# Fourier mix behind attention: later sines, another sign mask, sign changes on three engines, and one relay moved ahead

## The chip, the cores and the metric

The kernel runs on one core of a Trainium2 chip. The metric is the device time of one launch in microseconds (us). Its engines, as the profile names them, are TensorE (PE, its weight loads PEld), VectorE (DVE), ScalarE (ACT), GpSimd (POOL) and SyncE (SP); SP issues most of the plain stores and transposing DMAs, POOL the loads.

## The reference

Eight batches, twelve heads, 448 positions, head width 64:

```python
scores = scale * np.matmul(q, k.transpose(0, 1, 3, 2))
attn = np.maximum(scores, 0.0) ** 2 / S
x = np.matmul(attn, v)                 # heads side by side: (8, 448, 768)
u = x + np.real(np.fft.fft(np.fft.fft(x, axis=1), axis=2))
un = (u - mean(u)) / np.sqrt(var(u) + 1e-6)
out = u + np.maximum(un @ w_ch1, 0.0) @ w_ch2      # 768 -> 3072 -> 768
```

So there is an attention without softmax, a Fourier mix along positions and channels of which the real part is added, a normalization of each row, and a feed-forward part of two large products.

## The kernel before, in words

**Tiling.** Attention takes one batch after another, four heads to a group (`load_group`: q, k and v come by POOL's DMAs as bf16). For batches 0 and 1 queries and keys are turned on TensorE (`turn_on_pe`, L545 and the copy L552). From batch 2 on, DVE copies them into relay buffers `qkr` (L509), one buffer for queries and one for keys, and SP turns each by a transposing DMA into `qkT` (L521). The relay of one group is thus a q copy, a k copy and two DMAs; a relay buffer is free when its DMA has read it. Scores (L857) land in PSUM, ACT takes relu (L870) into an `sq` buffer, DVE squares it (L887; elsewhere ACT, L884), and TensorE multiplies by values (L842 in batch 0, L785 later). The result leaves PSUM as `xT` (L594 on ACT, L596 on DVE), and DVE folds each block of 128 channels with its mirror image (sum and difference, L671).

**Fourier mix.** The transforms are products with cosine and sine tables, built on the chip. For each table `turns` makes the phase as a fraction of a turn (L311, L313) and its absolute value (L315), on DVE; `sine` then has ACT take two sines (L320). There are two tables for positions (`seq`) and three for channels (`chan` 0, 1, 2); half of each channel table is needed with the sign changed, too (`chan_neg`, L361, and `nseq`, L357). In batch 0 `first_channels` multiplies six folded blocks of channels (m = 0 to 5) by the tables (L1307), in two row blocks i: blocks 0 to 2 use `chan[m]`, blocks 3 to 5 use `chan[m-3]` and `chan_neg`. Row block 1 waits for all scores of batch 0. The PSUM results are cast (`pc`, L1351), and `first_tail` does the position products (L932), the residual (L935), the statistics and the norms. Behind the last relu ACT loads another function table, for square roots (`root_table`, L367). Later batches go through `mix` (L1332, L1351) and `mix_rows` (L1147).

**Feed-forward part.** Rows are taken in groups; the first product is L1793 with a relu (L1778 DVE, L1780 ACT), the second L1821, L1848 and L1933, partly with sums of weight blocks, and L1515 adds onto the output rows. Two PSUM banks (`BF`) and three double banks (`BS`) serve all of it.

**Order of the work.** The program's order is made at build time by a planner (`Streams.run`). Each piece of work is a generator that asks with `need(engine, duration, waits, buffers)`, and issues its instructions when it is chosen. The planner always takes the piece that can start earliest by its own durations; on a tie, the smaller rank goes first, and the rank is a pair, one for TensorE and one for the other engines, given at `sch.add`. An `need("SP", 0.0, ...)` only waits in the plan and emits nothing. `warming` fills TensorE with matmuls on zeros (L2011) until batch 0's channel products are done. Each engine runs its instructions in the planned order, and waits in it for whatever its next instruction needs.

`turn_rest` plans the groups of batches 1 to 7 one after another at rank (2, 2). `others` builds channel tables 1 and 2, at 0.15 for DVE and ACT; squares have 0.2, `first_fold` 0.3, `negative` (nseq and the three sign changes) 0.35.

Of the kernel before, what the change touches and what calls it, by code (L numbers as in the profile page):

```python
# [166 lines left out]
def kernel(  # L167
# [9 lines left out]
    nc = tc.nc  # L177
# [125 lines left out]
    def build_dft():  # L303
        row, col, col2 = drow, dcol, dcol2

        def turns(f, g, cols, rows, n, i):

            d = dve(n) + 0.04
            yield need("DVE", d, [indices_ready])
            r = work.tile([128, 2 * KH], mybir.dt.int32, name="dftr", tag=f"pc{TC[i][0]}", bufs=1)  # L310
            nc.vector.tensor_scalar(r[:, :n], cols, rows, None, op0=ALU.mult)  # L311
# [3 lines left out]
            nc.vector.scalar_tensor_tensor(g, f, -1.0, f, op0=ALU.mult, op1=ALU.max)  # L315
            return e

        def sine(dst, y, n, e, sign=1, bias=zero_t):
            e = yield need("ACT", act(n), [e + LATENCY["DVE"]])
            nc.scalar.activation(dst, y, AF.Sin, bias=bias, scale=sign * 2.0 * math.pi)  # L320
            dft_ready.t = e + LATENCY["ACT"]
# [13 lines left out]
        def channel_table(m):  # L335
            y = early_hid if m == 2 else work.tile([128, 4 * KH], FP32, name="dfty", tag=("u1A", "u1B")[m], bufs=1)
            e = yield from turns(y[:, 2 * KH:4 * KH], y[:, 0:2 * KH], col2, row[:, 4 + m:5 + m], 2 * KH, m % 2)
            yield from sine(chan[m][:, 0, :], y[:, 0:2 * KH], 2 * KH, e, -1, halfpi)
            yield from sine(chan[m][:, 1, :], y[:, 2 * KH:4 * KH], 2 * KH, e)
            chan_made[m].t = dft_ready.t  # L340
# [10 lines left out]

    chan_made, dft_all = [Cell() for _ in range(3)], Cell()

    def negative():

        e = yield need("DVE", 0.35, [seq_ready])
        nc.vector.tensor_scalar(nseq, seq[:, 1], -1.0, None, op0=ALU.mult)  # L357
        nseq_ready.t = e + LATENCY["DVE"]
        for m in range(3):
            e = yield need("DVE", 0.27, [chan_made[m]])  # L360
            nc.vector.tensor_scalar(chan_neg[:, m], chan[m][:, :, KH:], -1.0, None, op0=ALU.mult)  # L361
            chan_ready[m].t = e + LATENCY["DVE"]

    def root_table():

        yield need("ACT", 1.5, [dft_all, last_relu])
        nc.scalar.activation(drow[:, 7:8], zero_t, AF.Sqrt, bias=eps_t)  # L367
# [128 lines left out]

    def turning(bs):

        for b in bs:
            for g in range(NG):  # L500
                if b < 2:
# [68 lines left out]
    def fold(b, m, F, av, give, av_end):  # L570
# [58 lines left out]
        if b == 0:  # L629
# [662 lines left out]

    first_pps, first_chan = [None, None], [Cell(), Cell()]

    def first_channels(i, ms):

        n0, n1 = TC[i]
        for m in ms:
# [4 lines left out]
            for t in range(2):  # L1303
                parts = [(0, 2 * KH, chan[m][:, t, :])] if m < 3 else \
                    [(0, KH, chan[m - 3][:, t, 0:KH]), (KH, 2 * KH, chan_neg[:, m - 3, t, :])]
                for c0, c1, tab in parts:
                    nc.tensor.matmul(first_pps[i][:n1 - n0, t, c0:c1], lhsT=first_folds[m][:, t, n0:n1], rhs=tab,  # L1307
                                     start=(i == 1 and m == 0), stop=(m == MC - 1 and c1 == 2 * KH))
        if m < MC - 1:
            sch.add(first_channels(i, [MC - 1]), (0, 0))  # L1310
        else:
# [704 lines left out]
    with tc.manual_schedule():  # L2016
# [18 lines left out]
        sch.add(root_table(), (0, 0.4))  # L2035
        sch.add(negative(), (0, 0.35))
        for slot in range(6):
# [33 lines left out]
```

## Time and profile before

| what | us |
|---|---|
| median of 3 runs (577.87 to 578.24) | 578.0 |
| the profiled execution | 577.99 |
| its span | 576.0 |
| TensorE busy | 565.0 |
| VectorE busy | 446.9 |
| ScalarE busy | 336.9 |
| GpSimd busy | 134.0 |

The span goes from the first to the last instruction of the profiled execution; its time has 1.99 us more around it. A row of a timeline reads: start, duration, engine, line, operation, output <- inputs, size, count, and in brackets how long the engine had been idle and what ended that. A merged row (x5) covers several instructions. Lines are those of the listing above.

### The profile page before, as it was taken

The numbers are of one execution on the slowest core, as the hardware profiler recorded it, in microseconds if no ns is written. First come the engines' busy times: TensorE is split into PE (matmuls) and PEld (weight loads), VectorE is DVE, ScalarE is ACT, GpSimd is POOL, SyncE is SP. The second block draws the span as 40 slices with busy tenths as digits, with TensorE's granted clock in tenths as the row PEclk, the third lists the DMA queues.
The fourth block names the chain that finished last, engine by engine and source line by source line (L and its number), as shares of the span: only waits on it lengthen the run. The fifth ranks groups of instructions, "written<-read, shape, count | busy, mean of one in ns | idle before, by whom it ended". The sixth has DMA issues, their size and how long they took to land.

```text
span 576.0 us, 11341 instructions
## 1 busy us (share of the span) xinstructions
PE 565.0 (98%) x4339; PEld 358.5 (62%) x4344; DVE 446.9 (78%) x1030; ACT 336.9 (59%) x538; POOL 134.0 (23%) x187
## 2 busy tenths in 40 slices
PE   8999999999999999999999999999999999999997
PEld 6466556544465546556757567568567786868864
DVE  6988775986688877997798879978978994267872
ACT  5977772977745676667559658856573160406400
POOL 8527102410134113321333116112220230000000
PEclk9999999999999999999999999999999999999999
DMA  9999999656938985799769977996654342223012
GB/s 125 206 211 249 202 219 181 174 109 78 202 78 223 175 140 119 161 167 193 140 136 197 201 126 161 177 173 113 141 107 94 109 142 85 66 73 93 2 41 97
DMA packets 133505, 81.84 MB, mean 142 GB/s; under 512 B 77516, under 2 KB 128716, under 8 KB 133452
## 3 DMA queue, kind: packets, MB, share of 16 engines
q0 software_dynamic: 40320, 33.63, 37.2%
q1 hardware_dynamic: 93132, 47.50, 36.6%
q8 instruction: 34, 0.56, 0.4%
q14 instruction: 19, 0.16, 0.1%
HBM read 62.91 MB, written 26.25 MB: 155 GB/s over the span
## 4 chain that ended last, share of the span: by engine, by line
PE 87%; DVE 9%; ACT 3%; issue 1%; DVEq 0%; ACTq 0%
PE psF L1793 31%; PE psF L1933 21%; PE psS L857 6%; PE psF L785 5%; PE psF L1821 4%; PE psS L1933 4%; PE psS L1635 3%; PE psF L1848 3%; PE psS L1332 2%; DVE sq L887 2%; ACT sq L870 1%; PE psS L785 1%; PE psS L2011 1%; PE psF L1635 1%; PE psS L932 1%; PE psS L1307 1%
## 5 line engine op out<-in xcount | busy, mean ns | idle before, releaser
L1793 PE MATMUL psF<-unT,w 128*128 128x256 bf16 (+2 forms) x1435 | 197.6, 294 | 1.3 <-ACT hT L1780 0.7
L870 ACT ACTIVATE sq<-psS 112x896 bf16<-112x896 f32 x192 | 165.2, 930 | 39.6 <-PE psS L857 39.2
L1793 PEld LDWEIGHTS <-w 128*128 128x128 bf16 x1440 | 137.5, 98 | 58.7 <-issue 12.9
L887 DVE TENSOR_TENSOR sq<-sq 112x896 bf16<-112x896 bf16 x163 | 98.4, 620 | 15.9 <-ACT sq L870 14.9
L1780 ACT ACTIVATE hT<-psF 128x512 bf16<-128x512 f32 (+3 forms) x144 | 71.7, 513 | 66.5 <-PE psF L1793 65.3
L1933 PEld LDWEIGHTS <-hT 128*128 128x128 bf16 x720 | 69.0, 98 | 50.3 <-issue 5.9
L1933 PE MATMUL psF<-w,hT 128*128 128x384 bf16 x378 | 67.1, 326 | 0.7 <-DVE xT L612 0.7
L1515 DVE TENSOR_TENSOR o<-psF,o 128x384 f32<-128x384 f32 x80 | 44.2, 553 | 25.2 <-PE psF L1933 20.8
L857 PE MATMUL psS<-qkT 64*128 64x448 bf16 (+1 forms) x384 | 52.8, 358 | 2.5 <-ACT sq L870 1.9
L413 POOL DMA_DIRECT2D vn<-in_v_dram x24 | 17.5, 730 | 105.4 <-PE psS L857 86.0
L1176 POOL TENSOR_TENSOR u<-tp,xn 112x385 f32<-112x385 f32 (+2 forms) x14 | 13.6, 974 | 109.0 <-DVE tp L1158 81.8
L857 PEld LDWEIGHTS <-qkT 64*128 64x128 bf16 (+1 forms) x384 | 17.3, 101 | 31.1 <-issue 24.1
L612 DVE TENSOR_SCALAR xT<-psF 128x224 bf16<-128x224 f32 x54 | 18.5, 383 | 21.8 <-PE psF L785 21.7
L785 PE MATMUL psF<-sq,vn 112*64 112x448 bf16 x264 | 31.3, 358 | 0.9 <-DVE hT L1778 0.9
L1204 ACT ACTIVATE un<-u,nmr,rstd 113x768 bf16<-113x768 f32 (+2 forms) x23 | 23.0, 1022 | 14.9 <-DVE nmr L1191 14.6
L413 POOL DMA_DIRECT2D qn<-in_q_dram x21 | 15.2, 724 | 62.7 <-DVE qkr L509 53.0
L1933 PE MATMUL psF<-wsum,hT 128*128 128x384 bf16 x162 | 28.8, 326 | 0.0
L1185 DVE BATCH_NORM_STATS2 stats<-u 112x6 f32<-112x384 f32 (+2 forms) x56 | 28.8, 540 | 0.0
L785 PEld LDWEIGHTS <-vn 112*64 112x64 bf16 x336 | 15.8, 109 | 19.6 <-issue 13.4
L884 ACT ACTIVATE sq<-sq 112x896 bf16<-112x896 bf16 x29 | 27.3, 950 | 0.5
L1821 PE MATMUL psF<-w,hT 128*128 128x384 bf16 x144 | 24.9, 326 | 0.0
L1848 PE MATMUL psF<-w,hT 128*128 128x384 bf16 x144 | 24.4, 326 | 0.0
(228 smaller groups left out, 783.2 us busy)
## 6 DMA issues: line engine op xcount, KB each, us to landing
out_dram<-o SPq DMA_DIRECT2D x56, 192.0 KB, 2.3
vn<-in_v_dram POOLq DMA_DIRECT2D x24, 224.0 KB, 5.0
qn<-in_q_dram POOLq DMA_DIRECT2D x21, 224.0 KB, 4.5
kn<-in_k_dram POOLq DMA_DIRECT2D x21, 224.0 KB, 7.3
w<-in_moe_w_ch_dram POOLq DMA_DIRECT2D x12, 384.0 KB, 13.2
w<-in_moe_w_ch_dram POOLq DMA_DIRECT2D x4, 1152.0 KB, 15.5
utop<-u SPq DMA_DIRECT2D x12, 336.0 KB, 3.8
o<-utop SPq DMA_DIRECT2D x16, 192.0 KB, 4.2
```

Source lines behind the costliest of these rows:

```text
L413: nc.gpsimd.dma_start(out=t, in_=src[b, hs].rearrange("h (p j) d -> p h (j d)", j=4))
L785: nc.tensor.matmul(av[h * Dh:(h + 1) * Dh, 0:S], lhsT=vn[:, c, h0 + h, :], rhs=sq[:, h, :], start=(c == 0), stop=(c == 3))
L857: nc.tensor.matmul(sc[:wide, h, 0:S].rearrange("k (c q) -> k c q", c=4), lhsT=flat[ps, k0:k0 + wide], rhs=qT[ps, m % 2], start=True, stop= ...
L870: nc.scalar.activation(r, sc[:R, :, 0:S], AF.Relu)
L887: nc.vector.tensor_tensor(r, r, r, op=ALU.mult)
L1185: nc.vector.bn_stats(stats[:n, hf, :], u[:n, hf * (D // 2):(hf + 1) * (D // 2)])
L1515: nc.vector.tensor_tensor(o, pc[:, 0:DH], o, op=ALU.add)
L1780: nc.scalar.activation(hs, ps, AF.Relu)
L1793: nc.tensor.matmul(ph[:, i * N:(i + 1) * N], lhsT=w1_sb[m][hf][:, (jj + i) * 128:(jj + i + 1) * 128], rhs=unT[:, m, 0:N], start=(m == 0), ...
L1821: nc.tensor.matmul(pc[:, 0:DH], lhsT=block(j, c), rhs=w2(j, hf), start=(j == 0), stop=(j == JC - 1))
L1848: nc.tensor.matmul(pc[:, 0:DH], lhsT=block(2 * i + k, c), rhs=weights[i], start=(start and i == 0), stop=(i == KP - 1), skip_group_check=True)
L1933: nc.tensor.matmul(pc[:, 0:DH], lhsT=lhs[i], rhs=rhs[i], start=(start and i == 0), stop=(i == KP - 1), skip_group_check=True)
```

## The change

- **Late sines.** Both sines of channel table 2 now also wait, in the plan, for the last relu of batch 0. The other tables' sines stay as they are.
- **Sign mask.** The absolute value of the phase is made by clearing the sign bit of the 32-bit word, an operation with one source, where it was the larger of f and −f. The planned durations change with it.
- **Moved sign changes.** `chan_neg` of table 0 stays on DVE, that of table 1 goes to POOL, that of table 2 to ACT, and the function table for square roots is loaded behind the latter. The rank of `negative` goes from 0.35 to 0.15.
- **Folds and channel products.** `first_fold` gets rank 0.2 for the engines other than TensorE. The channel products of batch 0 are planned as separate pieces: block 0, then blocks 1 to 4 in any order, and block 5 when these four are done.
- **Relay.** `turn_rest` plans batch 2's three groups one by one, each when the one ahead of it is turned. The second of them (batch 2, group 1) gets rank 0.05 for its copies, all others keep 2.

```diff
-            yield need("DVE", d, [indices_ready])
+            yield need("DVE", d - 0.14, [indices_ready])
...
-            e = yield need("DVE", d)
-            nc.vector.scalar_tensor_tensor(g, f, -1.0, f, op0=ALU.mult, op1=ALU.max)
+            e = yield need("DVE", dve2(n))
+            nc.vector.tensor_scalar(g.bitcast(mybir.dt.int32), f.bitcast(mybir.dt.int32), 0x7FFFFFFF, None, op0=ALU.bitwise_and)
...
-        def sine(dst, y, n, e, sign=1, bias=zero_t):
-            e = yield need("ACT", act(n), [e + LATENCY["DVE"]])
+        def sine(dst, y, n, e, sign=1, bias=zero_t, deps=()):
+            e = yield need("ACT", act(n), [e + LATENCY["DVE"], *deps])
...
+            deps = [last_relu] if m == 2 else []
+            yield from sine(chan[m][:, 0, :], y[:, 0:2 * KH], 2 * KH, e, -1, halfpi, deps)
+            yield from sine(chan[m][:, 1, :], y[:, 2 * KH:4 * KH], 2 * KH, e, deps=deps)
...
-            e = yield need("DVE", 0.27, [chan_made[m]])
-            nc.vector.tensor_scalar(chan_neg[:, m], chan[m][:, :, KH:], -1.0, None, op0=ALU.mult)
-            chan_ready[m].t = e + LATENCY["DVE"]
+            en = ("DVE", "POOL", "ACT")[m]
+            e = yield need(en, {"DVE": 0.27, "POOL": 0.7, "ACT": act(2 * KH)}[en], [chan_made[m]])
+            if en == "ACT":
+                nc.scalar.activation(chan_neg[:, m], chan[m][:, :, KH:], AF.Copy, scale=-1.0)
+                negated.t = e
+            else:
+                (nc.gpsimd if en == "POOL" else nc.vector).tensor_scalar(chan_neg[:, m], chan[m][:, :, KH:], -1.0, None,
+                                                                         op0=ALU.mult)
+            chan_ready[m].t = e + LATENCY[en]
...
-        yield need("ACT", 1.5, [dft_all, last_relu])
+        yield need("ACT", 1.5, [dft_all, last_relu, negated])
...
-        sch.add(turning(range(1, B)), (2, 2))
+        sch.add(turning([1], range(NG)), (2, 2))
+        yield need("SP", 0.0, [*turned_at[1][2]])
+        sch.add(turning([2], [0]), (2, 2))
+        yield need("SP", 0.0, [*turned_at[2][0]])
+        sch.add(turning([2], [1]), (2, 0.05))
+        yield need("SP", 0.0, [*turned_at[2][1]])
+        sch.add(turning([2], [2]), (2, 2))
+        yield need("SP", 0.0, [*turned_at[2][2]])
+        sch.add(turning(range(3, B), range(NG)), (2, 2))
...
-            sch.add(first_fold(m, x, f, gone.t + LATENCY["DVE"]), (0.3, 0.3))
+            sch.add(first_fold(m, x, f, gone.t + LATENCY["DVE"]), (0.3, 0.2))
...
-        if m < MC - 1:
-            sch.add(first_channels(i, [MC - 1]), (0, 0))
+        if m == 0:
+            for x in range(1, MC - 1):
+                sch.add(first_channels(i, [x]), (5, 5))
+        elif m < MC - 1:
+            channels_made[i] += 1
+            if channels_made[i] == MC - 2:
+                sch.add(first_channels(i, [MC - 1]), (0, 0))
...
-            sch.add(first_channels(i, range(MC - 1)), (5, 5))
+            sch.add(first_channels(i, [0]), (5, 5))
...
-        sch.add(negative(), (0, 0.35))
+        sch.add(negative(), (0, 0.15))
```

More of the change, by code (lines that the diff above doesn't have):

```diff
@@ L350, in build_dft @@
         sch.add(others(), (0, 0.15))
-    chan_made, dft_all = [Cell() for _ in range(3)], Cell()
+    chan_made, dft_all, negated = [Cell() for _ in range(3)], Cell(), Cell()
     def negative():
@@ L495, with turning @@
     turned_at = [[[Cell() for _ in range(2)] for _ in range(NG)] for _ in range(B)]
-    def turning(bs):
+    def turning(bs, gs=range(NG)):
         for b in bs:
-            for g in range(NG):
+            for g in gs:
                 if b < 2:
```

4 lines of the change are left out of this document (1 added, 3 removed).

## The prediction

> **What bounds the kernel now.** I read the page's busy line first, then the shares of the chain that ended last.
>
> ```profile
> PE 565.0 (98%) x4339; PEld 358.5 (62%) x4344; DVE 446.9 (78%) x1030; ACT 336.9 (59%) x538; POOL 134.0 (23%) x187
> ...
> PE 87%; DVE 9%; ACT 3%; issue 1%; DVEq 0%; ACTq 0%
> ```
>
> TensorE is busy nearly throughout, so the next view is the table of stages, TensorE alone (stretch, its length, busy time and instructions, granted clock, DMA share, GB/s), from the first feed-forward work on.
>
> ```profile
> 48.00:72.00 24.00, 22.35 (x214) 1.00 1.19 222
> 72.00:240.00 168.00, 167.72 (x1096) 1.00 0.84 154
> 240.00:348.00 108.00, 107.33 (x839) 1.00 0.91 164
> 348.00:360.00 12.00, 11.07 (x102) 1.00 0.83 182
> 360.00:528.00 168.00, 167.89 (x1323) 1.00 0.54 118
> ```
>
> In these 480 us TensorE idles 1.65 + 0.28 + 0.67 + 0.93 + 0.11 = 3.64 us, at a full granted clock. What remains is work that no part of the change removes. A gain must come from the opening, before useful TensorE work is dense (there its busy time holds filler matmuls of L2011), or out of those 3.64 us. So I read the opening, by all engines, then the timelines of ACT, DVE and PE one by one.
>
> ```profile
> 24.00:36.00 12.00, 11.07 (x74) 5.48 (x74) 11.78 (x34) 10.80 (x17) 4.08 (x7) 1.00 1.08 212
> ```
>
> The columns are PE, PEld, DVE, ACT and POOL. DVE is busy 11.78 of 12 us here. ACT's 10.80 us understate it:
>
> ```profile
> 22.12 0.73 ACT L320 ACTIVATE chan<-early,halfpi 128x386 bf16<-128x386 f32 x1
> 22.62 0.72 ACT L320 ACTIVATE chan<-early,zero_t 128x386 bf16<-128x386 f32 x1
> 23.13 6.67 ACT L870 ACTIVATE sq<-psS 112x896 bf16<-112x896 f32 x8
> ...
> 32.06 1.16 ACT L870 ACTIVATE sq<-psS 112x896 bf16<-112x896 f32 x1
> 33.24 1.28 ACT L367 ACT_TABLE_LOAD   x1
> 34.53 0.29 ACT L367 ACTIVATE drow<-zero_t,eps_t 128x1 f32<-128x1 f32 x1
> 36.90 1.05 ACT L1351 CAST pc<-psS 128x386 bf16<-128x386 f32 x2 [2.08 <-PE psS L1307]
> ```
>
> No row before the last carries an idle time: ACT runs without a gap through batch 0's last relu, which ends by 33.24, and only then idles, 2.08 us, for TensorE's first channel products (L1307). What comes behind that relu:
>
> ```profile
> 33.25 0.62 DVE L887 TENSOR_TENSOR sq<-sq 112x896 bf16<-112x896 bf16 x1
> 33.79 0.65 DVE L671 TENSOR_TENSOR fold<-xT 128x225 bf16<-128x225 bf16 x3
> 34.35 0.37 DVE L361 TENSOR_SCALAR channeg<-chan 128x386 bf16<-128x386 bf16 x1
> 34.64 0.67 DVE L596 TENSOR_SCALAR xT<-psF 128x224 bf16<-128x224 f32 x2
> 35.23 0.42 DVE L361 TENSOR_SCALAR channeg<-chan 128x386 bf16<-128x386 bf16 x2
> 35.57 0.45 DVE L671 TENSOR_TENSOR fold<-xT 128x225 bf16<-128x225 bf16 x2
> ```
>
> and TensorE, first its timeline, then two pieces of the chain that ended last:
>
> ```profile
> 34.03 0.38 PE L842 MATMUL psF<-sq,vn 112*64 112x448 bf16 x2
> ...
> 35.12 0.24 PE L1307 MATMUL psS<-channeg,fold 128*128 128x193 bf16 x1
> 35.20 0.25 PE L1307 MATMUL psS<-chan,fold 128*128 128x193 bf16 x1
> ```
> ```profile
> 34.41 2.79 PE psS L1307 x28
> 37.20 0.51 PE psF L545 x16
> ```
>
> Last relu, square (L887), last values (L842), x turned out of PSUM (L596), last fold (L671) follow each other; but TensorE still has 28 of the channel matmuls to do behind the last values, back to back to 37.20. They could not come sooner: five of the twelve folds and all three sign changes stand at the end of DVE's queue. Two things bound the opening, ACT's sum up to the last relu and this backlog.
>
> **The change, part by part.** *Late sines.* Channel table 2's two sines leave the relu run and follow the last relu. By the starts of the rows they hold ACT for 23.13 − 22.12 = 1.01 us, so the last relu ends at 33.24 − 1.01 = 32.23, if DVE frees the buffers as fast. They then run at 32.23 and 32.73 and end at 32.73 + 0.69 = 33.42 (0.69 from the row of table 1's second sine, below).
>
> *Sign mask.* `|f|` becomes a one-source operation.
>
> ```profile
> 18.42 0.69 ACT L320 ACTIVATE chan<-dfty,zero_t 128x386 bf16<-128x386 f32 x1
> ```
> ```profile
> 16.79 0.55 DVE L315 SCALAR_TENSOR_TENSOR dfty<-dfty 128x386 f32<-128x386 f32 x1
> ...
> 19.10 0.41 DVE L311 TENSOR_SCALAR dftr<-dcol,drow 128x386 int32<-128x386 f32 x1
> ```
>
> The nearest row is L311, one source of the same size: 0.41 for 0.55 us. No row has a bitwise operation; the saving lies between 0 and, at half the old price, 0.28 us an operation. I take 0.14. Of five, two stand in the full stretch behind 14 us: 0.28 us of DVE.
>
> *Moved sign changes.* Table 0's stays on DVE but goes ahead of squares. Table 1's goes to POOL, table 2's to ACT: DVE loses one or both of the 35.23 pair, which held it to 35.57, 0.34 us for two.
>
> ```profile
> 39.54 0.48 ACT L984 COPY u<-psS 128x384 f32<-128x384 f32 x1 [0.82 <-DVE stats L955]
> ```
> ```profile
> 29.88 0.53 POOL L443 DMA_DIRECT2D w<-in_moe_w_ch_dram  x1 [1.28 <-DMA w<-in_moe_w_ch_dram]
> ...
> 43.29 0.99 POOL L1005 TENSOR_SCALAR un<-u,rstd,nmr 128x768 bf16<-128x768 f32 x1 [0.76 <-DVE nmr L976]
> ```
> ```profile
> L1793 PE MATMUL psF<-unT,w x144: 322/326/337, 51.7 to 88.0; 128*128 128x384 bf16 x144
> ...
> DMA to landing us min/median/max: 6.7/13.2/19.3
> ```
>
> On ACT, L984's 0.48 us is the price (it reads PSUM; 0.3 to 0.7 bound it by DVE's 0.37 and the sine's 0.69). On POOL, L1005 handles twice the elements in 0.99 us, so between 0.5 and 1.0; I take 0.6. It waits for table 1's sines (done at 19.11), with first-weight loads queued behind it. The cover is the ring of DMAs: the load at 29.88 stood 1.28 us for an earlier one. Without it the last load lands 1 us later than 29.88 + 13.2 = 43.1; its first reader starts at 51.7. Nothing, either way.
>
> *Folds and channel products.* Folds tie with squares instead of losing to them, and the products of channel blocks 1 to 4 become separate, in any order, behind block 0. No instruction is added: 36 matmuls as before, 0.08 us apiece for the narrow ones (35.20 − 35.12), 0.16 for the wide. With folds and table 0's sign early, blocks 0, 1, 3, 4 go into time that holds filler. Behind the last values stay block 5 (eight narrow ones, 0.66 us) and block 2 (four wide, 0.65 us), which fits before it. DVE must do these folds, up to 0.65 us, before the last square; against that stand 0.28 us of masks and its small idle. It may lag ACT by up to 0.4 us.
>
> *The sum.* Square 32.26 to 32.88. From the rows: values 0.16 us behind it (34.03 − 33.87), x 0.61 us behind their start, fold 0.93 − 0.34 = 0.59 behind that, so 34.24 to 34.69; block 5 is done about 35.45. On ACT: sines to 33.42, sign change to 33.95, table load 1.28 to 35.23, square-root 0.29 to 35.52. Both paths let the first cast start near 35.5, against 36.90: 1.4 us at most. The least: the backlog stays, and only the values come 1.01 − 0.4 = 0.6 us sooner. I choose 1.3, since both paths agree near the top. The table load lay under 2.08 us of idle; that cover is now gone, and ACT is next late.
>
> The Trainium skill ("ScalarE: Activation LUTs", What ACT_TABLE_LOAD costs) adds to such a load a drain of some 1.38 us. Here the load's row is 1.28 us and the square root starts 0.01 us behind its end, so the trace does not show that drain on this side.
>
> *Relay.* Batch 2's second queries and keys, copied by DVE (L509) and turned by DMA, now go ahead of all DVE work; the four planning steps on SP emit nothing, and its DMAs are the same six.
>
> ```profile
> 94.23 1.03 DVE L1351 CAST pc<-psS 97x772 bf16<-97x772 f32 x1 [2.98 <-PE psS L1332]
> 95.21 0.56 DVE L1515 TENSOR_TENSOR o<-psF,o 128x384 f32<-128x384 f32 x1
> 95.68 0.42 DVE L509 COPY qkr<-qn 112x1024 bf16<-112x1024 bf16 x1
> 98.29 0.43 DVE L509 COPY qkr<-kn 112x1024 bf16<-112x1024 bf16 x1 [2.19 <-DMA qkT<-qkr]
> ```
>
> The key copy stops DVE 2.19 us for the previous group's transpose, and yet the table has TensorE idle 0.28 us in all of 72 to 240. If the pair moves up past the add of 95.21, that add ends near 99.2 and returns its bank late; DVE was idle 2.98 us just before, so a cast or add is what it can pass. I take 0 and keep +3.8 (below); below nothing, at most the 0.28 us.
>
> **Rivals.** *A, later waits eat it.* The opening's shift changes every later choice of the planner. Against: the stages are dense. For: some are left, and a new one the size of the present 0.67, 0.93 or 1.65 us costs that much. 576.7 + 0.7 to 1.7 gives 577.4 to 578.4, say 577.9.
>
> *B, the relay stops the mix: slower.* The mechanism is the wait above, placed one instruction earlier, ahead of the cast at 94.23. Then the cast runs after 98.72 and ends near 99.75, and TensorE meets its readers:
>
> ```profile
> 95.98 1.49 PE L1147 MATMUL psS<-pc,seqm 128*128 128x385 bf16 x8
> ```
>
> They would start 3.8 us late, with all TensorE work behind them in order: 578.0 − 1.3 + 3.8 = 580.5 if the transpose moves forward with the rest, 581.8 if the DMAs keep their hours. It decides once the pair stands ahead of the cast and the transpose lands later than the cast's inputs, by more than 1.3 us. For: the transpose does land late, at 98.29. Against: the pair stands behind cast and add today, so its buffers were planned free no sooner.
>
> *C, the new plan also closes waits.* Of 3.64 us perhaps a third, 1.2: 575.5.
>
> *D, the opening moves little.* ACT becomes the bound: today 2.08 us of idle follow the square root, so a cost of the table load that its row doesn't show could lie hidden there, anything from 0 to 2.08 us. With two thirds of it the first cast starts at 36.9 again, 578.0. Against: the square root's row begins 0.01 us behind the load's. Or DVE lags and the backlog stays: 577.4.
>
> By the page named above, the hidden part would be its drain, and the time 578.0 too.
>
> **How the numbers follow.** The profiled execution took 577.99 us, its span 576.0 with 1.99 around; the median is 578.0, so the sum needs no correction. Forecast: 578.0 − 1.3 = **576.7**, own range 575.9 to 577.3, chance 0.41; A 0.22; B 0.24 (partial stalls from 579.2 up included); C 0.08; D 0.05. The range of 8 in 10 runs from **575.2 to 580.4**: half of B and half of C, 0.16, lie outside. It has both signs, for B is near in chance.
>
> 0.2% (about what a measurement of this kernel can tell from no change) is 1.16 us. The forecast lies just past that bound, at 576.84; of its 0.41 some 0.09 fall short. Faster: 0.32 + C = 0.40. Same: 0.09 + A + D = 0.36. Slower: B, 0.24.
>
> **What would show it.** Last relu ending near 32.2 with table 2's sines behind it, and the table load behind a Copy; `|f|` near 0.4 us; one channeg on DVE, before 20 us; L1307 spread over the time before the last values, with a remainder near 1.3 us where 2.79 stood; the first pc cast near 35.5 to 36.0. After that, TensorE's idle time from 48 to 528 near 3.6 us. Wrong would be: a relu run that ends at 33 because DVE holds it; an ACT that keeps the casts waiting past 36; an idle TensorE ahead of L1147 and a DVE waiting over 2.2 us on qkT near 92 to 97; or new waits of 0.7 us and more in stages now dense.

## The result, and the profile after

The changed kernel takes 585.18 us, median of six runs (583.34 to 595.24), against 578.13 us of the kernel before in the same series; the ratio is 1.0112 with a 95% interval of 1.0087 to 1.0136. The forecast of 576.7 us was wrong in its sign, and the time lies above the range of 575.2 to 580.4. The profiled execution of the changed kernel took 585.11 us, its span 583.2. In some executions the granted clock is lower and the time some 2% longer (the 595.24 us, clock 0.968): the medians count them, the ratios (but for x1's below) do not, and the profiled executions of x1 and y1 were of that kind, so of these two only the times are used.

From its page, the busy line and the shares of the chain that ended last:

```profile
PE 565.9 (97%) x4330; PEld 357.7 (61%) x4330; DVE 444.6 (76%) x1024; ACT 332.6 (57%) x537; POOL 143.6 (25%) x194
...
PE 81%; DMA 8%; DVE 6%; ACT 3%; issue 1%; POOL 0%; SPq 0%; DVEq 0%; POOLq 0%; ACTq 0%
```

TensorE has as much work as before in a longer span, and a share of 8% of the chain is now DMA, of which the chain of before had none. Where the time went is read from the table of stages, TensorE alone: stretch, its length, busy time and instructions, granted clock, DMA share, GB/s. The changed kernel:

```profile
36.00:48.00 12.00, 11.67 (x132) 1.00 1.13 227
48.00:72.00 24.00, 20.92 (x191) 1.00 1.22 214
...
84.00:96.00 12.00, 8.74 (x58) 0.86 1.57 146
...
108.00:168.00 60.00, 58.60 (x377) 1.00 0.81 139
...
228.00:252.00 24.00, 22.12 (x143) 1.00 1.00 186
```

The kernel before, in the stretches that the prediction didn't quote:

```profile
36.00:48.00 12.00, 11.84 (x135) 1.00 1.16 222
...
84.00:96.00 12.00, 12.00 (x90) 1.00 1.41 166
...
108.00:168.00 60.00, 59.74 (x371) 1.00 0.72 120
...
228.00:252.00 24.00, 23.34 (x156) 1.00 0.78 157
```

The opening did what was forecast, and more. The changed kernel's ACT timeline:

```profile
31.54 0.61 ACT L320 ACTIVATE chan<-early,halfpi 128x386 bf16<-128x386 f32 x1
...
32.68 0.52 ACT L364 ACTIVATE channeg<-chan 128x386 bf16<-128x386 bf16 x1
33.22 1.28 ACT L374 ACT_TABLE_LOAD   x1
34.52 0.30 ACT L374 ACTIVATE drow<-zero_t,eps_t 128x1 f32<-128x1 f32 x1
35.18 1.05 ACT L1371 CAST pc<-psS 128x386 bf16<-128x386 f32 x2 [0.37 <-PE psS L1322]
```

The last relu ends by 31.54, the sines, the sign change and the table load follow without a gap, and the first cast starts at 35.18 instead of 36.90: **1.72 us gained**. Then the balance of the stages, idle time of the changed kernel less that of before:

| what | us |
| --- | --- |
| first cast earlier, 36.90 to 35.18 | −1.72 |
| 36 to 48: 0.33 idle for 0.16 | +0.17 |
| 48 to 72: 3.08 for 1.65 | +1.43 |
| 84 to 96: 3.26 for 0 | +3.26 |
| 84 to 96: lower clock (below) | +1.77 |
| 108 to 168: 1.40 for 0.26 | +1.14 |
| 228 to 252: 1.88 for 0.66 | +1.22 |
| 348 to 360: 0 for 0.93 | −0.93 |
| all other stretches up to 528 | +0.38 |
| sum | +6.72 |

The two profiled executions differ by 585.11 − 577.99 = 7.12 us; 0.40 us of it has no place in the table. So the gain is nearly gone at 72 us (−0.12), and the largest loss is one place, 84 to 96 us.

Of the 3.08 us that TensorE idles at 48 to 72 us, 1.23 are waits for loads, of which the kernel before had none there: it stands for the queries and keys of batch 1's last group. Its timeline in the changed kernel:

```profile
58.94 0.39 PE L552 MATMUL psF<-ident,qn 112*64 112x112 bf16 x8 [0.47 <-DMA qn<-in_q_dram]
60.08 0.39 PE L552 MATMUL psF<-ident,kn 112*64 112x112 bf16 x8 [0.76 <-DMA kn<-in_k_dram]
```

and the same two loads in the kernel before (KB, us from issue to landing):

```profile
qn<-in_q_dram POOLq DMA_DIRECT2D x1, 224.0 KB, 6.1
kn<-in_k_dram POOLq DMA_DIRECT2D x1, 224.0 KB, 6.4
```

Before, they were issued at 51.19 and 51.99, landed at 57.3 and 58.4 and were read at 57.90 and 59.30, in time by 0.6 and 0.9 us. The changed kernel issues them 2.15 us earlier, at 49.04 and 49.84, and yet they land only near 58.9 and 60.0, 1.6 us later than before. The opening's shift of 1.72 us met margins that were smaller than itself.

For 84 to 96 us, the changed kernel's chain:

```profile
57.49 31.77 DMA qn<-in_q_dram
...
89.35 0.43 DVE qkr L516
89.78 0.61 DVE xT L627 x2
...
93.46 2.77 PE psS L1352 x24
```

and DVE's timeline, then TensorE's:

```profile
84.41 0.39 DVE L678 TENSOR_TENSOR fold<-fold,seqm 128x450 bf16<-128x450 bf16 x1
89.35 0.43 DVE L516 COPY qkr<-qn 112x1024 bf16<-112x1024 bf16 x1 [4.55 <-DMA qn<-in_q_dram]
```
```profile
90.44 3.02 PE L1813 MATMUL psF<-unT,w 128*128 128x384 bf16 x12 [3.26 <-DVE xT L627]
93.25 0.69 PE L1352 MATMUL psS<-chan,fold 128*128 128x193 bf16 x3
...
95.82 0.41 PE L1352 MATMUL psS<-chan,diff 128*97 128x193 bf16 x3
```

This is a queue that stops at its head. DVE came to the relay copy of batch 2's first queries at 84.8 and stood 4.55 us for a load that was not there. Behind the copy stood the turn of batch 1's x out of PSUM (L627), whose inputs were ready; TensorE needed its bank and stood 3.26 us. After that the clock was lower for a while. The same groups in the chain of z1 (below), where nothing stops:

```profile
67.13 3.03 PE psF L1813 x18
...
88.99 2.00 PE psS L1352 x24
```

Twelve of L1813 take 12 / 18 of 3.03 = 2.02 us there and 3.02 here, the 24 of L1352 2.00 and 2.77: 1.00 + 0.77 = 1.77 us.

Why was the load not there? DMA issues of queries and keys of batch 2's first group (KB, us to landing), in the kernel before, then in the changed one:

```profile
qn<-in_q_dram POOLq DMA_DIRECT2D x1, 224.0 KB, 28.1
kn<-in_k_dram POOLq DMA_DIRECT2D x1, 224.0 KB, 29.4
```
```profile
qn<-in_q_dram POOLq DMA_DIRECT2D x1, 224.0 KB, 31.8
```

and POOL's timelines with their issues and DVE's copies of before, then POOL's of the changed kernel:

```profile
55.89 0.78 POOL L413 DMA_DIRECT2D qn<-in_q_dram  x1
56.60 0.77 POOL L413 DMA_DIRECT2D kn<-in_k_dram  x1
...
86.08 0.42 DVE L509 COPY qkr<-qn 112x1024 bf16<-112x1024 bf16 x1
86.41 0.42 DVE L509 COPY qkr<-kn 112x1024 bf16<-112x1024 bf16 x1
```
```profile
56.24 0.83 POOL L461 DMA_DIRECT2D w<-in_moe_w_ch_dram  x1 [3.28 <-DMA w<-in_moe_w_ch_dram]
57.49 0.72 POOL L420 DMA_DIRECT2D qn<-in_q_dram  x1 [0.41 <-PE psF L1813]
```

Before, the loads landed at 55.89 + 28.1 = 84.0 and 56.60 + 29.4 = 86.0, and the copies came at 86.08 and 86.41, without an idle time on their rows: they were in time by 2.1 and **0.4 us**. In the changed kernel DVE reached the copy at 84.8 us, 1.3 ahead of before, and the load landed 5.3 us later, since it was issued 1.6 us later (POOL stood 3.28 us for an earlier weight load) and took 3.7 us longer. The DMA engines are full in both: busy shares of 1.13 to 1.57 from 36 to 96 us.

### The profile page after: what moved, and what is told of

It reads as the page before. It is cut to its first block, busy times and chain, and to the rows that moved or that the text cites. A ratio compares the mean times of both kernels' runs of the same rounds, so it can differ in the third digit from the quotient of the medians.

```text
span 583.2 us, 11320 instructions
## 1 busy us (share of the span) xinstructions
PE 565.9 (97%) x4330; PEld 357.7 (61%) x4330; DVE 444.6 (76%) x1024; ACT 332.6 (57%) x537; POOL 143.6 (25%) x194
## 4 chain that ended last, share of the span: by engine, by line
PE 81%; DMA 8%; DVE 6%; ACT 3%; issue 1%; POOL 0%; SPq 0%; DVEq 0%; POOLq 0%; ACTq 0%
PE psF L1813 26%; PE psF L1953 22%; DMA qn<-in_q_dram 5%; PE psS L872 5%; PE psF L1841 4%; PE psF L800 4%; PE psS L1953 4%; PE psF L1868 3%; PE psS L1655 3%; PE psS L1352 3%; DVE sq L902 2%; DMA qkT<-qkr 2%; ACT sq L885 2%; PE psS L800 2%; PE psF L1655 1%
## 5 line engine op out<-in xcount | busy, mean ns | idle before, releaser
L1813 PE MATMUL psF<-unT,w 128*128 128x256 bf16 (+2 forms) x1440 | 198.8, 295 | 6.4 <-DVE xT L627 3.3
L1813 PEld LDWEIGHTS <-w 128*128 128x128 bf16 x1440 | 137.9, 98 | 63.7 <-issue 14.7
L1800 ACT ACTIVATE hT<-psF 128x512 bf16<-128x512 f32 (+3 forms) x153 | 76.7, 518 | 77.9 <-PE psF L1813 76.0
L902 DVE TENSOR_TENSOR sq<-sq 112x896 bf16<-112x896 bf16 x166 | 103.6, 638 | 16.4 <-ACT sq L885 15.4
L627 DVE TENSOR_SCALAR xT<-psF 128x224 bf16<-128x224 f32 x50 | 17.0, 382 | 18.5 <-PE psF L800 18.4
L899 ACT ACTIVATE sq<-sq 112x896 bf16<-112x896 bf16 x26 | 24.5, 949 | 0.3
L1664 ACT COPY copies<-psS 128x256 f32<-128x256 f32 x30 | 10.7, 373 | 21.1 <-PE psS L1655 19.8
## 6 DMA issues: line engine op xcount, KB each, us to landing
w<-in_moe_w_ch_dram POOLq DMA_DIRECT2D x12, 384.0 KB, 15.2
```

The source lines that it names most:

```text
L902: nc.vector.tensor_tensor(r, r, r, op=ALU.mult)
L1800: nc.scalar.activation(hs, ps, AF.Relu)
L1813: nc.tensor.matmul(ph[:, i * N:(i + 1) * N], lhsT=w1_sb[m][hf][:, (jj + i) * 128:(jj + i + 1) * 128], rhs=unT[:, m, 0:N], start=(m == 0), ...
```

## The experiments

Theory: **loads and transposes keep their hours** while the DMA engines are full (they land at about the same time, whatever TensorE does), so an opening that ends earlier only makes TensorE and DVE arrive too early at batch 1's and batch 2's queries and keys; and DVE's in-order queue turns a late load into idle TensorE time where other work stands behind the copy. Rivals: the relay's new order is the cause; POOL's sign change, which delays loads, is; the late sines are; or the planner, which orders everything anew after any change, has simply drawn a worse order.

| run | median, us | ratio to before, 95% interval |
| --- | --- | --- |
| x1_old_relay | 593.49 | 1.0249, 1.0210 to 1.0289 |
| x2_landed_rows | 587.50 | 1.0170, 1.0152 to 1.0187 |
| x3_sign_on_dve | 585.19 | 1.0130, 1.0113 to 1.0147 |
| x4_relay_only | 578.19 | 1.0002, 0.9992 to 1.0012 |
| y1_after_light | 582.03 | 1.0064, 1.0040 to 1.0088 |
| y2_before_light | 579.19 | 1.0005, 0.9988 to 1.0022 |
| y3_handed_back | 585.06 | 1.0115, 1.0093 to 1.0136 |
| y4_loads_first | 588.51 | 1.0164, 1.0103 to 1.0226 |
| z1_after_late_plan | 580.73 | 1.0040, 1.0019 to 1.0061 |
| z2_before_late_plan | 591.39 | 1.0217, 1.0181 to 1.0254 |
| z3_early_sines | 582.13 | 1.0056, 1.0028 to 1.0084 |
| z4_late_sines_only | 578.16 | 0.9999, 0.9982 to 1.0017 |
| w1_light_late_plan | 580.03 | 1.0030, 1.0016 to 1.0043 |
| w2_margin_12 | 585.79 | 1.0129, 1.0093 to 1.0165 |
| w3_margin_14 | 578.17 | 1.0002, 0.9993 to 1.0011 |
| v1_light_margin_14 | 576.27 | 0.9967, 0.9953 to 0.9981 |
| v2_loads_first_14 | 586.79 | 1.0146, 1.0117 to 1.0175 |

### The relay: x1 and x4

x1 is the changed kernel with the old relay:

```diff
-        sch.add(turning([1], range(NG)), (2, 2))
...
-        sch.add(turning(range(3, B), range(NG)), (2, 2))
+        sch.add(turning(range(1, B)), (2, 2))
```

> The changed kernel with the relay planned as before (batches 1 to 7 in a row, all at rank 2). Theory 'loads keep their hours': the first group's copies stand where they stood, so DVE still waits about 4.6 us for the load and TensorE 3.3 us near 87; the time stays within 2 us of 585, depending on later waits. Theory 'relay': the time falls to 576 to 578.

x4 is the kernel before with the new relay, the same diff turned round.

> The kernel before with the relay part alone. Theory 'loads keep their hours': the opening is untouched, the load is waited for as little as before, and the time stays within 1.5 us of 578. Theory 'relay': 2 us or more are lost.

Measured: x1 593.49 us, some 8 us slower still, where up to 2 had been expected; x4 578.19 us, a ratio of 1.0002. The relay by itself is not the cause. In the order of before it costs and gains nothing; taking it out of the changed kernel has everything behind it planned anew, and that plan is worse.

### The wait itself: x2 and x3

x2 takes away what DVE waited for: the two copies of batch 2's first group read rows of the first weights, which landed long before. The order is the same on every engine.

```diff
-                    nc.vector.tensor_copy(o, loads[b * NG + g][x])
+                    nc.vector.tensor_copy(o, loads[b * NG + g][x] if b * NG + g != 2 * NG else
+                                          w1_sb[x][0][:R, 0:1024].rearrange("p (h j d) -> p j h d", h=4, j=4))
```

> The two relay copies of batch 2's first group read rows of the first weights, which landed long before, instead of the loaded queries and keys (so batch 2's first four heads get wrong scores); every instruction keeps its place on every engine. Theory 'loads keep their hours': DVE no longer stands 4.6 us for the load of queries, the turning of x behind it comes 3 us sooner, TensorE loses its 3.26 us of idle time between 87 and 90 and the 1.8 us that its clock at 0.86 cost behind it: 585.2 - 5 = about 580 us, unless a later wait takes some back. Theory 'relay': the cost lies in the second group's pair; nothing or under 1 us is gained. Theory 'sign on POOL delays loads': gains like the first, since it shares the wait.

Measured: 587.50 us, not faster. At 84 to 96 us TensorE is full now (12.00 of 12), but batch 2's scores then wait for the transposing DMA behind the copy. TensorE, and the piece of the chain ahead of it, in x2:

```profile
102.25 1.30 PE L872 MATMUL psS<-qkT 64*128 64x448 bf16 x6 [5.36 <-DMA qkT<-qkr]
```
```profile
90.65 11.56 DMA qkT<-qkr
```

The key copy was done at 86.73, and its transpose still landed at 102.2. Two things stood between. In SP's queue the transposes of batch 1's x stand ahead of it, and by the profile the last of them waits for a fold on DVE; SP's row behind them:

```profile
88.66 5.62 SPq L528 DMA_TRANSPOSE qkT<-qkr  x2
```

So the keys' transpose, the second of this row, was issued at 90.65 only, and from then on it took 11.56 us. I had taken the copy's wait for the whole cost, 5 us; the wait moved 12 us down the same chain. In the changed kernel the first scores ran at 102.36, without a wait on their row, in x2 at 102.25. The chains of other runs show how far the hour is the DMA's: the transpose of these keys was issued at 85.79 (y4), 89.21 (v2) and 92.48 (x3) and landed at 98.65, 101.98 and 102.27, so an issue 6.7 us earlier landed 3.6 us earlier. The kernel before has the queries' transpose issued at 86.66, ahead of the last transpose of x; that SP's new order costs the changed kernel time was not tested.

x3 puts table 1's sign change from POOL back on DVE.

```diff
-                (nc.gpsimd if en == "POOL" else nc.vector).tensor_scalar(...)
+                nc.vector.tensor_scalar(...)
```

> The sign change of channel table 1 is issued on DVE at its planned place instead of POOL; nothing else moves. Theory 'loads keep their hours': POOL issues batch 1's second loads 2.0 us sooner (from 13.8 to about 11.8), but the DMA engines were loaded anyway, so the load of batch 2's first queries lands at most 1 us earlier than 89.3 and the time falls by 0 to 1 us. Theory 'sign on POOL delays loads': the 1.61 us on POOL and its wait are the delay; the load lands 2 us or more earlier, and 2 to 4 us are gained.

Measured: 585.19 us, no change, as the first theory has it. The load lands 0.7 us earlier, at 88.65, and TensorE waits twice (x3's rows):

```profile
89.73 2.12 PE L1813 MATMUL psF<-unT,w 128*128 128x384 bf16 x12 [3.69 <-DVE xT L627]
...
102.43 0.74 PE L872 MATMUL psS<-qkT 64*128 64x448 bf16 x6 [2.37 <-DMA qkT<-qkr]
```

Here the clock did not fall (12 matmuls in 2.12 us), and yet the first scores begin at 102.43 again, after a second wait of 2.37 us. What was gained ahead of the transposes is lost at them.

### Fewer loads, and a gain handed back: y1, y2, y3, y4

y1 fills the second half of the first weights with a constant instead of loading it, six loads of 384 KB fewer. y2 is the same in the kernel before.

```diff
-            nc.gpsimd.dma_start(
+            nc.gpsimd.memset(t, 0.02) if hf else nc.gpsimd.dma_start(
```

> The changed kernel, every instruction at its place, but the second half of the first weights is filled by POOL with a constant instead of loaded (that half of the first product is computed with the constant): six loads of 384 KB less, some 2.3 MB or 10 us of DMA time before 90 us. Theory 'DMA hours' (the loads and transposes up to about 100 us set when batch 2's first scores can begin, whatever TensorE does): the copy of batch 2's first queries no longer waits, nor do the scores for their transpose; TensorE's idle time from 48 to 108 falls by 4 us or more, its clock stays at 1.0, and the time falls by 5 us or more, to 580 or less. Theory 'order' (the re-planned order itself is worse): TensorE still idles, the time stays above 582.

> The same edit on the kernel before, as the control. Both theories: TensorE hardly waits for DMAs there, so under 1 us is gained, 577 to 578. With 'DMA hours', the changed kernel with this edit is 0 to 2 us faster than this one, as its opening is 1.7 us shorter; with 'order', it is 4 us or more slower.

Measured: y1 582.03 us, y2 579.19. Fewer loads are worth about 3 us in the changed kernel (ratio 1.0064 for 1.0112) and nothing in the kernel before. 5 us or more had been expected of the loads, so this lies between the two theories: with the same lighter loads the changed kernel is still slower than the kernel before (1.0064 against 1.0005), and that part belongs to its order.

y3 hands the opening's gain back: two copies hold ACT behind the square root.

```diff
         nc.scalar.activation(drow[:, 7:8], zero_t, AF.Sqrt, bias=eps_t)
+        for _ in range(2):
+            nc.scalar.copy(early_hid[:, 0:900], early_hid[:, 0:900])
```

> The changed kernel with two copies of 900 elements on ACT (about 1.8 us, no one reads them anew) behind the square-root load, so that the first cast starts near 37.0 as before instead of 35.2: the opening's gain is handed back, no order changes. Theory 'DMA hours': the gain was worth nothing, the waits for loads shrink by what the opening grows; 584 to 586. Theory 'order' or a plain sum: every us of the opening counts, 587.

Measured: 585.06 us. The first cast in y3's ACT timeline, then its stages:

```profile
36.48 1.04 ACT L1373 CAST pc<-psS 128x386 bf16<-128x386 f32 x2
```
```profile
48.00:72.00 24.00, 22.18 (x211) 1.00 1.20 221
84.00:96.00 12.00, 11.40 (x85) 1.00 1.43 168
96.00:108.00 12.00, 9.88 (x54) 0.86 0.98 224
```

The first cast is 1.30 us later than in the changed kernel, and the time is the same. 1.26 us of it came back at 48 to 72 us alone (22.18 busy for 20.92), and the wait at 84 shrank to 0.60, with 2.12 us of waiting for a transpose and a lower clock at 96 to 108 in its place. So in this order the opening's gain is worth nothing.

y4 issues batch 2's first queries and keys ahead of the last two parts of the second weights.

```diff
+        yield from load_group(2 * NG, (0, 1))
         yield from load_w2(range(2, 4))
-        for i in range(2 * NG, B * NG):
+        yield from load_group(2 * NG, (2,))
+        for i in range(2 * NG + 1, B * NG):
```

> The changed kernel with the loads of batch 2's first queries and keys ahead of the last two quarters of the second weights; the planner re-plans all behind it. Theory 'DMA hours': the load lands near 75 instead of 89, DVE doesn't wait for it, but the transposes still share the DMA engines with the weights; between 579 and 584. Theory 'order': no better than 585 on purpose, only by chance.

Measured: 588.51 us, above the expected 579 to 584. The planner, which had the loads earlier, put the copies earlier too: DVE stood 6.88 us for a transpose ahead of the key copy, and 96 to 108 us held 8.44 us of TensorE work at a clock of 0.72.

### The planner's margin: z1, z2, w2, w3

The planner takes batch 2's queries and keys for ready 9 us behind their modelled landing. z1 sets 16, w2 12, w3 14, in the changed kernel; z2 sets 16 in the kernel before. The planner then places these copies later, and all that follows anew.

```diff
-            ready[i][x].t = landed[-1] + (1.5 if g else 0.0, 3.0, 9.0, 5.0)[min(b, 3)]
+            ready[i][x].t = landed[-1] + (1.5 if g else 0.0, 3.0, 16.0, 5.0)[min(b, 3)]
```

> The changed kernel, but the planner takes batch 2's queries and keys for ready 16 us instead of 9 us behind their modelled landing (the profile of the changed kernel has the first of these loads land 31.8 us after its issue). DVE's copies of them then stand behind the turns of x and the last batch-1 fold, not ahead of them. Theory A, that the loss comes in two parts, hours of DMA that no order of TensorE's work can move and a DVE queue that stops behind a load that is not there yet: the second part goes, TensorE has useful work at 84 to 96 us (over 11.5 us busy where the changed kernel has 8.74), batch 2's scores still wait for the transposes, and the time is 579 to 582 us. Theory B, that DMA alone decides and the wait merely moves: 584 to 587 us. Theory C, that the loss sits in the later waits (156 to 168, 228 to 252 us): 584 us or more with 84 to 96 us full.

> Control: the same planner's margin of 16 us in the kernel before. There the copies waited for no load (rows at 86.08 and 86.41 us, loads landed 84.0 and 86.0). Theory A and B: nothing to gain, 577.5 to 579.5 us. If it is below 577 us, the margin is a gain of its own; if over 581 us, the later batch-2 scores themselves cost and the run above has to be read against this one.

> The changed kernel with a margin of 12 us for batch 2's queries and keys instead of 9 or 16. The copies stand behind batch 1's last pair of casts of the channel product, near where the 16 us put them, but the plan differs from there on. Theory A: 84 to 96 us is full, and the time is that of the kernel before (the opening's gain used up at 48 to 72 us) plus the waits that this plan happens to have behind 100 us: 578 to 582 us. Rival, that the margin of 16 us was a lucky draw and the copy's place is not the cause: 584 us and more with 84 to 96 us full.

> The same with a margin of 14 us; again another plan behind 100 us. Theory A: 578 to 582 us, 84 to 96 us full; what stands above 578 us lies in waits behind 100 us that can be named. Rival: 584 us and more with 84 to 96 us full. Below 577 us: the opening's gain does reach the end in some order, against theory A.

z1: 580.73 us, 4.4 less than the changed kernel. Its stages:

```profile
48.00:72.00 24.00, 21.28 (x192) 1.00 1.21 215
...
84.00:96.00 12.00, 12.00 (x89) 1.00 1.31 149
...
168.00:228.00 60.00, 57.11 (x386) 1.00 0.93 168
```

The copies stand behind the last x and the casts of batch 1, as intended, and 84 to 96 us is full (11.93 of 12 behind it). Its balance against before: first cast at 35.48, −1.42; 48 to 72 us +1.07; a new 2.89 at 168 to 228, where DVE and a transpose are late; the other stretches −0.49; sum 2.05, measured 580.18 − 577.99 = 2.19 for the profiled executions.

w3: 578.17 us, the time of the kernel before. Its first cast is at 35.16, and behind 108 us no wait was added:

```profile
48.00:72.00 24.00, 21.66 (x196) 1.00 1.21 213
...
96.00:108.00 12.00, 11.09 (x79) 1.00 1.25 250
```

−1.74 at the opening, +0.19 at 36 to 48 us, +0.69 at 48 to 72, +0.89 at 96 to 108 (batch 2's scores wait 0.91 us for `qkT`, again at 103.28): the sum is 0.03, the profiled executions differ by 577.39 − 577.99 = −0.60. Of the 1.74, 0.48 us are a wait for keys at 48 to 72 us and 0.91 the wait for the transpose, which SP issued only at 96.62, behind a store of output rows; what remains is about equal to before. That is the theory's case.

w2: 585.79 us. That contradicts my expectation and fits the rival's: 84 to 96 us is full, and yet it is slow.

```profile
168.00:228.00 60.00, 56.72 (x371) 0.97 0.87 162
...
252.00:348.00 96.00, 93.73 (x732) 1.00 0.93 167
```

Its largest loss lies at 168 to 348 us, 3.28 + 2.27 of idle time and a lower clock. And z2, the kernel before with a margin of 16, takes 591.39 us where 577.5 to 579.5 had been expected, with all of 72 to 108 us full; its first long wait is at 192 to 216 us (18.76 us busy of 24, the clock 0.86 in the first half and 0.71 in the second), with a DMA of 7.34 us into `unT` in its chain. So z1's 4.4 us can't be put down to the copies' place alone. The margin is no remedy: each planning draws its own waits behind 100 us. What holds is narrower: with the copies late the wait at 84 to 96 us is gone in all three, and the one order that then has no added waits behind 108 us comes out at the time of before, not below.

### The opening's parts: z3 and z4

z3 is the changed kernel with table 2's sines back among the relus and all sign changes on DVE; z4 is the kernel before with the late sines alone.

```diff
-            deps = [last_relu] if m == 2 else []
+            deps = []
...
-            en = ("DVE", "POOL", "ACT")[m]
+            en = ("DVE", "DVE", "DVE")[m]
```

> The changed kernel with channel table 2's sines back among the relus and all three sign changes on DVE; the sign mask, the earlier folds, the split channel products and the relay's order stay. Theory A: what hurts is that useful work reaches batch 2's loads too early; the opening loses about 1 us of its gain, first cast near 36 us, so the wait at 84 to 96 us gets shorter but the time stays within 583 to 586 us, as with the two copies that handed the opening's gain back. Rival, that the late sines themselves (or the sign changes on POOL and ACT) cost what was lost: 578 to 580 us.

> The kernel before with one edit: channel table 2's two sines wait for the last relu. The last relu ends 1.0 us earlier, near 32.2 us; the backlog of channel products on TensorE stays, so the first cast comes at 36.0 to 36.9 us. Theory A: a gain of 0 to 0.6 us at the opening reaches the end in full or not at all, 577.5 to 579 us, unless the plan puts batch 2's copies earlier against their loads: then 580 us and more, with the wait for a load of queries in DVE's queue near 85 us. Rival (late sines are the cost): 583 us or more without such a wait.

z3: 582.13 us (577.75 to 585.06), first cast at 36.11; between the two cases. Its loss is at 96 to 108 us (9.13 us busy, clock 0.86), behind a transpose of 10.03 us. z4: 578.16 us, ratio 0.9999; the first cast moves from 36.90 to 36.53 only, since the backlog on TensorE stays. Late sines alone neither gain nor cost. No run has the sign mask, or the folds and channel products, alone.

### Whether the gain can pass at all: w1 and v1, and a last try

w1 is z1 with the lighter weights of y1, v1 is w3 with them; order as in z1 and w3.

> The run with the 16 us margin (580.7 us), and beside it the second half of the first weights filled with a constant instead of loaded, so 6 loads of 384 KB fewer; the order on TensorE and DVE is the same as in that run. Theory A (the opening's gain is used up at 48 to 72 us, where TensorE waits for the loads of queries and keys): those 24 us hold over 22.3 us of TensorE work where the run with the margin holds 21.28, and the time falls by 1.0 to 1.8 us, to 579 to 579.8 us; the waits of 168 to 228 us, which are DVE's, stay near 2.9 us. Rival, that loads do not set 48 to 72 us: no change, 580.2 to 581.2 us.

> The run with the 14 us margin (578.17 us, the same as the kernel before), with the second half of the first weights filled with a constant instead of loaded; the order on every engine is that of the 14 us run. There TensorE had 2.34 us idle at 48 to 72 us and 0.91 at 96 to 108, against 1.65 and 0.02 in the kernel before: 1.58 us that ate the opening's 1.74. Theory A, that these are hours of loads: with fewer loads most of it goes, over 22.2 us busy at 48 to 72 us, first scores of batch 2 no longer behind a transpose, and the time falls by 0.8 to 1.6 us, to 576.5 to 577.4 us, below the kernel before for once. Rival, that the opening's gain cannot pass in any case: 577.8 to 578.6 us.

w1: 580.03 us; 22.08 us busy at 48 to 72 us where z1 has 21.28, less than I expected, and the intervals of w1 and z1 overlap: inconclusive, as 2.99 us at 168 to 228 stayed. v1: **576.27 us, ratio 0.9967**, 0.9953 to 0.9981, below the kernel before, which with the same lighter loads gained nothing (y2), and a little below the expected 576.5 to 577.4. Its first cast is at 35.15; its stages:

```profile
48.00:72.00 24.00, 22.08 (x197) 1.00 1.08 173
...
96.00:108.00 12.00, 12.00 (x87) 1.00 1.03 242
```

0.42 us more at 48 to 72 than w3 (22.08; I had asked for 22.2), with no wait for a load there, and no wait for a transpose at 96 to 108. The order is the same in both, so here the loads alone decide: with 2.25 MB of them less the gain passes to the end, and what w3 lacked was DMA time.

v2 tries the same with the work complete: w3's margin, and y4's order of loads.

> A try at a version that beats both kernels, complete in its work: the margin of 14 us, and batch 2's first queries and keys loaded ahead of the last two parts of the second weights, so that they land some 10 us sooner. If the new plan has no long wait behind 100 us, theory A gives 576.8 to 578 us; but the order is planned anew, and the plans so far had 0 to 6 us of waits there, so up to 584 us. Rival (the opening's gain cannot pass): not below 577.8 us.

Measured: 586.79 us, above all that was expected. Batch 2's first scores waited 5.34 us for their transpose and began at 102.03, near where they began in the changed kernel. The loads were earlier, the transposes not: SP had issued the keys' at 89.21, again behind transposes of batch 1's x, and it took 12.77 us. No complete version beat the kernel before; w3 equals it.

## Why the prediction was wrong

*Late sines.* Right, and low: last relu ended by 31.54 (forecast 32.23). With late sines alone (z4) the sines behind it start at 31.93, so some 0.4 us of this came from the other parts.

*Sign mask.* Right within its bounds: 0.36 to 0.55 us for `|f|` of 386 elements (0.41 taken). But all five ran by 13.4 us, so the 0.28 us that the forecast took out of DVE's full stretch behind 14 us were not there to gain.

*Moved sign changes.* ACT's 0.52 lies in its bounds. POOL's took 1.61 us, outside 0.5 to 1.0, at 12 us and not behind 19:

```profile
12.21 1.61 POOL L367 TENSOR_SCALAR channeg<-chan 128x386 bf16<-128x386 bf16 x1 [0.41 <-ACT chan L320]
```

x3 shows that this did not decide the time. The Trainium skill ("GPSIMD Engine Reference", 4.1 Engine selection) has one-input operations on this engine at roughly line rate; the trace differs, 1.61 us against 0.27 for the same change on DVE in the same kernel. L1020, of twice the elements, took 0.98 us on POOL, so the forecast's scaling by size was wrong; why is not shown.

*Folds, channel products, the sum at the opening.* Right in mechanism and near in size: first cast at 35.18 for the forecast 35.5. ACT was done at 34.82, and TensorE's last products decided, by 0.37 us. Behind the last values stood 20 products of some 2.1 us and not 1.3; 12 of them ran ahead of the last fold, as the forecast had block 2 do, so they cost nothing. The table load showed nothing hidden, as the square root starts 0.02 us behind its end; the drain of the Trainium skill ("ScalarE: Activation LUTs", What ACT_TABLE_LOAD costs) is not seen here either, and rival D fell.

*Relay.* A cost of 0 was right for this part alone (x4). Rival B had a DVE copy that stops the mix of batch 1. That is the right engine, but the wrong instruction: not the second pair behind a transpose at 94 us, but the first pair behind its load at 84, which the relay's new order leaves at its old priority. That its price came near (+3.8, for a wait of 3.26 and 1.77 of lower clock) is chance.

**The step that failed** is the one from the opening to the end, 578.0 − 1.3 = 576.7: it takes TensorE's work behind the opening to move forward whole, and puts waits for loads at nothing. Its one check was this: "Without it the last load lands 1 us later than 29.88 + 13.2 = 43.1; its first reader starts at 51.7. Nothing, either way." I looked at the margin of the first weights, 8.6 us, and at no other load. The loads that TensorE and DVE meet next had almost none: batch 1's last queries and keys 0.6 and 0.9 us, batch 2's keys 0.4 us. The stages table had said so beside the busy time I read, with a DMA share of 1.19 at 48 to 72. Busy TensorE at 72 to 108 us meant that loads came just in time, not that they could come sooner. The gain was used up by 72 us in the changed kernel and by 108 us in w3 (with fewer loads it passes, v1), and DVE's earlier arrival at 84.8 us met a load that landed later than before: the stop of 3.26 + 1.77 us.

Rival A said that the opening's shift redraws the planner's later choices; right in kind, far too small in price: I allowed 0.7 to 1.7 us for one new wait, the runs showed from 0.9 (w3) to more than 10 us (z2, where the opening didn't even move), and in the changed kernel 5.03 at 84 to 96 and 2.36 in two later stretches. In the first of these, TensorE stands 1.40 us ahead of 162.51 for a fold, which stood in DVE's queue behind a copy that waited for a transposing DMA; the changed kernel's chain:

```profile
154.88 4.81 DMA qkT<-qkr
```

In the second, 228 to 252 us, it stands three times, 0.51, 0.92 and 0.45 us, for relus and for x on DVE and ACT.

Three things stay open: why the load of queries took 3.7 us longer in the changed kernel, beyond POOL's 1.6 us later issue; how much of the late transposes is SP's order of issue and how much full DMA engines; and why some orders have long waits behind 150 us. No run isolated any of them. So what used up the opening's gain is shown (v1 against w3); why the changed kernel's order lost some 7 us on top is read from its trace, and x2, which removed the largest wait, did not bring the time back.

## What to carry to other kernels

Ahead of crediting a shorter opening, take each load and each DMA transpose that later work reads, and set its landing (issue plus time to landing of that issue, not a median over the program) against its first reader: as long as that landing does not move, the smallest margin is the most that can pass. Where DMA is full and the margin is under the gain, forecast no gain, and price what stands behind the reader in its engine's queue. Where a planner writes the order anew after any edit, add its scatter to the range (here 0 to 13 us), and test an edit in several orders before it is judged.

## What the hardware showed that was not expected

- A sign change of 128x386 bf16 on GpSimd took 1.61 us (1.43 to 1.60 in eleven more runs), against 0.52 on ScalarE and 0.27 on VectorE (0.25 to 0.68 for single ones in the runs).
- The clock after a stop: 3.26 us of idle TensorE were followed by groups of three L1352 matmuls of 0.69 us, and only from 95 us on by groups of 0.41 us; x3's stop of 3.69 us was followed by none of it. The Trainium skill ("TensorE: Matmul & The Clock Gate", Part 1: The HAM clock gate) has half the clock after an idle window of about 3.4 us that runs freely, so that, by it, the same stop can be caught or missed. The trace agrees in that one was and the other not, and its extra 1.77 us is near the 1.7 us estimated from one such window at half speed. It does not agree in the length: 3.26 us is shorter than that window, and in y3 a stop of 2.12 us was enough (18 of L1843 in 4.78 us behind it, in 3.09 ahead of it).
- With the DMA engines at busy shares over 1, a transposing DMA of 112x1024 elements took 10 to 12.9 us from issue to landing (z3, x2, v2, y4; 4.8 us near 155 us in the changed kernel), and a load of 224 KB 28 to 32 us in the kernel before and the changed one, where the medians over all loads of queries or keys are 4.5 to 7.3 us. With the last two weight loads issued behind it (y4, v2) the load of keys took 15.5 and 15.2 us.
